# Where 1,024 masked row-maximum instructions put their element-wise result: back into PSUM, or into one SBUF tile

## The chip, the cores and the metric

The kernel runs on one core of a Trainium2 chip. The metric is the device time of one execution in microseconds (us), taken as the median of several executions. A profile of one further execution gives every engine's instructions with their start and duration: PE (TensorE matmuls), PEld (its weight loads), DVE (VectorE), ACT (ScalarE), POOL (GpSimd) and SP (SyncE, which issues most DMAs).

## The reference, cut to what matters

Two layers, each an attention block and a feed-forward block on a sequence of 2048 rows with 640 features:

```python
x = A_x
for layer in range(2):
    x = x + attention(layernorm(x))   # 32 heads of 20; row i sees keys i-255 .. i
    x = x + mlp(layernorm(x))         # 640 -> 1536, relu(.)**2, -> 640, with biases
```

`attention` is softmax(mask(q k^T) / sqrt(20)) v, then a 640x640 projection. The softmax subtracts each row's maximum over its allowed keys. It is these maxima that the change touches.

## The kernel before

**Units.** The sequence is cut into 8 blocks of 256 rows; with two layers that makes 16 units, 0 to 15. Units 0 and 8 are the first of a layer and have no previous block of keys. Each unit goes through stages: layer norm and transposition, q and k (`stage_qk`), v (`stage_v`), attention, output projection (`stage_o`), second layer norm, feed-forward (`stage_f`). The dense stages of the unit before and the unit after are interleaved with the attention of the current unit, so that PE always has something to do.

**Attention.** The 32 heads go in 8 groups of four, called quads. For a quad `max_quad` (L617) first computes raw scores into two PSUM tiles `bb0` and `bb1` of three banks each (PE L653, or L668 in units 0 and 8). Then DVE adds the mask and takes the row maxima: eight reductions (L633), for four pieces w and, within each, for the two tiles e = 0 and 1 in turn. Such a reduction is one `tensor_tensor_reduce`; the profile shows it as two instructions, CUSTOM_DVE_ANT_0 (the pass over the scores, 128x320 in most units, 128x128 and 128x256 in units 0 and 8) and DVE_READ_ACCUMULATOR2_ANT (128x1, which writes the maximum into the small tile `mx`). Before the change the pass wrote the masked scores back over the raw ones, in place. Nothing reads them afterwards: only `mx` is used.

Later `exp_quad` (L737) computes transposed scores into the same two PSUM tiles (PE L757, or L765 where the unit is 0 or 8), with the row maxima included as extra rows of `qt`; ACT takes the exponentials (L779) into `pt`, POOL zeroes the masked corners (L794, L798), and `pv_quad` (L814) multiplies by v (PE L828). `max_quad` runs three quads ahead of `exp_quad`. So the two PSUM tiles change hands all the time: maxima of one quad, exponentials of another, maxima again.

**From the maxima to `qt`.** After every second quad the 16 columns of `mx` are turned into rows. In units 0 and 1 `max_out` (L715) transposes them on PE (L721), and DVE splits them into two half-precision parts in the tile `mT` (L726, L727). From unit 2 on `max_cross` (L694) splits them into `mh` on DVE (L704, L705), and a transposing DMA on SP (L709) makes the tile `mt`. Four small DMAs (L689) then carry the rows into `qt`.

**Order.** Each engine runs its own instructions in the order in which the program issues them. That order is written by a planner inside the kernel: `post` gives every job an engine, a cost in ns, and the jobs that it depends on; `pump` issues a job when its planned start has come. The plan takes 113 + 1.047 ns per column for a reduction (448 ns for 320 columns), whatever it writes. `banks` (L598) makes the next user of the two score tiles wait, in the plan, for all jobs on them, and dense matmuls fill PE's time until then. Accumulators of the dense stages (`acc`), of `pv` and of transposes share two further PSUM banks (`mm_tile`, L228): a matmul group cannot begin until ACT and DVE have emptied the bank it takes. Semaphores between engines, and between instructions of one engine, are not written in the kernel: the tile framework derives them from which instructions read and write which tile.

**SBUF tiles.** Tiles with the same tag share their buffers; a tile that takes over a buffer waits for the last readers of the one before it.

Of the kernel before, what the change touches and what calls it, by code (L numbers as in the profile page):

```python
# [11 lines left out]
F16 = mybir.dt.float16  # L12
BF16 = mybir.dt.bfloat16
# [3 lines left out]
P = 128  # L17
Q = P // 2
# [27 lines left out]
def kernel(ctx: ExitStack, tc: tile.TileContext, x, wqkv, wo, w1, b1, w2, b2, out):  # L46
    nc = tc.nc
# [3 lines left out]
    sb = ctx.enter_context(tc.tile_pool(name="sb", bufs=1))  # L51
# [81 lines left out]
    def post(eng, cost, fn, *deps, wait=0.0, prio=1, **kw):  # L133

        j = Job(eng, cost, fn, [d for d in deps if d is not None], now[0] + wait, prio, **kw)
        k = len(pend)
        while k and pend[k - 1].prio > prio:
            k -= 1
        pend.insert(k, j)
        return j  # L140
# [5 lines left out]
    def dma(fn, size, *deps, n=1, cost=450.0, prio=1, **kw):  # L146

        return post("S", n * cost, fn, *deps, prio=prio, size=size, **kw)
# [18 lines left out]
    def need(*js):  # L167

        for j in js:
            while j.end is None:  # L170
                pass_time()
            now[0] = max(now[0], j.end)
# [55 lines left out]
    def mm_tile(shape, name):  # L228


        while len(banks2) > 1:
            empty = [b for b in banks2 if b and all(j.end is not None for j in b)]
            if empty:
                b = min(empty, key=lambda b: max(j.end for j in b))
                now[0] = max(now[0], max(j.end for j in b) + LAT)
                banks2.remove(b)
            else:
                pass_time()
        t = ps.tile(shape, F32, name=name, tag="mm", bufs=2)
        banks2.append([])  # L240
        return t, banks2[-1]
# [350 lines left out]
    for m in mhs:  # L592
        nc.vector.memset(m, 0.0)

    bbjobs = []
    bb6 = [ps.tile([P, 3, 512], F32, name=f"bb{e}") for e in range(2)]

    def banks():  # L598
        need(*bbjobs)
        bbjobs.clear()  # L600
        return bb6

    def quarters(u):

        return u % NG != 0

    def by_tiles(pieces):

        at, order = {}, []
        for k, (tile, cols, put) in enumerate(pieces):  # L610
            order.append((at.get(tile, 0), k, put))
            at[tile] = at.get(tile, 0) + cols
        for _, _, put in sorted(order, key=lambda o: o[:2]):
            for e in range(2):
                put(e)

    def max_quad(n):  # L617

        u, qd = divmod(n, NQ)
        g = u % NG  # L620
        qt, cur, prev = qts[u], kts[u % 3], kts[(u - 1) % 3]
        G = qd // GQ
        if (u, G) not in mxs:
            mxs[u, G] = sb.tile([P, 2, 2 * GQ, 2], F32, name="mx", bufs=2)
        mx = mxs[u, G]
        need(trips[u, 0, qd], trips[u, 1, qd])
        bb = banks()

        accum = {(e, w): mx[:, e, (2 * qd + w // 2) % (2 * GQ), w % 2:w % 2 + 1] for e in range(2) for w in range(4)}

        def reduce(e, w, v, mask, cols):
            bbjobs.append(post("D", 113 + 1.047 * cols, lambda:
                               nc.vector.tensor_tensor_reduce(out=v, in0=v, in1=mask, scale=1.0, scalar=-3.0e38,  # L633
                                                              op0=ALU.add, op1=ALU.max, accum_out=accum[e, w]),
                               prio=urgency["turn"]))

        if quarters(u):
            flat = [b.rearrange("p a n -> p (a n)") for b in bb]
            pieces = []
            for w in range(4):  # L640
                j, i = divmod(w, 2)
                p, at = 2 * qd + j, 5 * Q * w
                cuts = sorted({0, 5 * Q, *(z - at for z in (512, 1024) if 0 < z - at < 5 * Q)})
                for o0, o1 in zip(cuts, cuts[1:]):
                    for h in range(2):
                        for kt, lo, hi, to in ((prev, 0, T - i * P, i * P), (cur, T - i * P, 3 * P, i * P - T)):
                            a, b = max(lo, o0 + h * Q), min(hi, o1 + h * Q)
                            if a >= b:
                                continue

                            def put(e, kt=kt, a=a, b=b, to=to, h=h, p=p, i=i, o=at + a - h * Q):
                                r, rows = slice(64 * e, 64 * e + 3 * DH), slice(64 * h, 64 * (h + 1))
                                nc.tensor.matmul(flat[e][rows, o:o + b - a], qt[r, p, i * P + 64 * h:i * P + 64 * (h + 1)],  # L653
                                                 kt[r, p, a + to:b + to], start=True, stop=True,
                                                 tile_position=(64 * e, 64 * h))

                            pieces.append((h, b - a, put))
            by_tiles(pieces)
            now[0] += 763.0
            for w in range(4):  # L660
                for e in range(2):
                    reduce(e, w, flat[e][:, 5 * Q * w:5 * Q * (w + 1)], maskq, 5 * Q)
        else:
            for w in range(4):
                j, i = divmod(w, 2)
                for e in range(2):
                    r, p = slice(64 * e, 64 * e + 3 * DH), 2 * qd + j
                    nc.tensor.matmul(bb[e][:, w % 3, w // 3 * T:w // 3 * T + (1 + i) * P], qt[r, p, i * P:(i + 1) * P],  # L668
                                     cur[r, p, :(1 + i) * P], start=True, stop=True)
            now[0] += 440.0  # L670
            for w in range(4):
                j, i = divmod(w, 2)
                for e in range(2):
                    to = bb[e][:, w % 3, w // 3 * T:w // 3 * T + (1 + i) * P]
                    if i:
                        reduce(e, w, to, maskw, 2 * P)
                    else:
                        reduce(e, w, to, maskw[:, P:], P)
        mxjobs[u, G] = list(bbjobs)
# [3 lines left out]
    def rows_out(qt, G, mT, ready):  # L683

        def spread():
            for e in range(2):
                for a in range(2):
                    r = 64 * e + 3 * DH + a
                    nc.sync.dma_start(qt[r:r + 1, 2 * GQ * G:2 * GQ * (G + 1), :].rearrange("p n (i m) -> p (n i) m", i=2),  # L689
                                      mT(e, a))  # L690

        return dma(spread, 16384, ready, n=4, cost=600.0, prio=0)

    def max_cross(u, G):  # L694

        mx, jobs = mxs.pop((u, G)), mxjobs.pop((u, G))
        NR = 8 * GQ
        box = {}

        def split():  # L700
            flat = mx.rearrange("p e n i -> p (e n i)")
            box["m"] = whole = mhs[G % 2]
            m = whole[:, :2 * NR].rearrange("p (a n) -> p a n", a=2)
            nc.vector.tensor_scalar(m[:, 0], flat, -1.0 / MS, None, op0=ALU.mult)  # L704
            nc.vector.scalar_tensor_tensor(m[:, 1], flat, -1.0 / MS, m[:, 0], op0=ALU.mult, op1=ALU.subtract)  # L705

        def turn():
            box["t"] = sb.tile([P, P], F16, name="mt", bufs=1)
            nc.sync.dma_start_transpose(box["t"], box["m"])  # L709

        j = post("D", 220, split, *jobs, prio=0)
        j = dma(turn, P * 2 * NR * 2, j, cost=1250.0, land=CROSS, prio=0)
        rowjobs[u, G] = rows_out(qts[u], G, lambda e, a: box["t"][a * NR + e * NR // 2:a * NR + (e + 1) * NR // 2, :], j)

    def max_out(u, G):  # L715

        qt, mx = qts[u], mxs.pop((u, G))
        NR = 8 * GQ
        need(*mxjobs.pop((u, G)))
        tr, jobs = mm_tile([P, 4, P], "tr")  # L720
        nc.tensor.transpose(tr[:NR, 0, :], mx.rearrange("p e n i -> p (e n i)"), ident)  # L721
        now[0] += 220.0
        mT = sb.tile([NR, 2, P], F16, name="mT", bufs=1)

        def rows():
            nc.vector.tensor_scalar(mT[:, 0], tr[:NR, 0, :], -1.0 / MS, None, op0=ALU.mult)  # L726
            nc.vector.scalar_tensor_tensor(mT[:, 1], tr[:NR, 0, :], -1.0 / MS, mT[:, 0],  # L727
                                           op0=ALU.mult, op1=ALU.subtract)

        j = post("D", 520, rows, prio=0)  # L730
        jobs.append(j)
        rowjobs[u, G] = rows_out(qt, G, lambda e, a: mT[4 * GQ * e:4 * GQ * (e + 1), a, :], j)
# [551 lines left out]
```

## Time and profile before

| | |
|---|---|
| time, median of 3 executions | 1586.17 us (1585.07 to 1589.79) |
| the profiled execution's own time | 1588.33 us |
| its span, first to last instruction | 1586.6 us |
| granted TensorE clock over the span | 0.995 |
| DVE instructions of L633 | 1,024 passes, 1,024 accumulator reads |

The profile's page gives for each engine the time it was busy and its share of the span. A row of the groups reads: line, engine, operation, output tile and input tile, shapes, count, then the total busy time, the mean duration of one instruction in ns, and the idle time of the engine just ahead of these instructions with what ended it. A row of the timeline reads: start in us from the span's start, duration in us, engine, line, operation, tiles, count, and in brackets an idle gap ahead of it with what ended that gap. Neighbouring instructions of the same form are merged into one timeline row. A duration includes any time in which the instruction was already in the engine behind another one, so two rows of one engine can overlap.

### The profile page before, as it was taken

The numbers are of one execution on the slowest core, as the hardware profiler recorded it, in microseconds if no ns is written. First come the engines' busy times: TensorE is split into PE (matmuls) and PEld (weight loads), VectorE is DVE, ScalarE is ACT, GpSimd is POOL, SyncE is SP. The second block draws the span as 40 slices with busy tenths as digits, with TensorE's granted clock in tenths as the row PEclk, the third lists the DMA queues.
The fourth block names the chain that finished last, engine by engine and source line by source line (L and its number), as shares of the span: only waits on it lengthen the run. The fifth ranks groups of instructions, "written<-read, shape, count | busy, mean of one in ns | idle before, by whom it ended". The sixth has DMA issues, their size and how long they took to land. (4 is left out here: it accounts for less than half of the span.)

```text
span 1586.6 us, 52541 instructions
## 1 busy us (share of the span) xinstructions
PE 1558.1 (98%) x21570; PEld 1168.7 (74%) x21570; DVE 984.7 (62%) x3254; ACT 734.3 (46%) x1593; POOL 600.3 (38%) x1291
## 2 busy tenths in 40 slices
PE   8899999999999999999999999999999999999989
PEld 7666777777777777777777777777778777676767
DVE  8776665666756656565566656657665666756532
ACT  4455545444454444535443453444535345354512
POOL 1233534235253443524324252442525325254512
PEclk9998999999999999999999999999999999999999
DMA  9764343362533525354352534535343343431020
GB/s 272 191 181 117 77 107 86 96 131 55 122 87 103 111 57 127 78 124 90 91 132 64 121 87 110 104 70 128 68 125 83 97 111 69 114 87 58 29 67 18
DMA packets 243353, 160.44 MB, mean 101 GB/s; under 512 B 91176, under 2 KB 226856, under 8 KB 243112
## 3 DMA queue, kind: packets, MB, share of 16 engines
q1 hardware_dynamic: 236744, 147.58, 38.8%
q10 hardware_dynamic: 6368, 9.50, 2.1%
q8 instruction: 169, 2.77, 0.7%
q14 instruction: 72, 0.59, 0.1%
HBM read 84.68 MB, written 52.95 MB: 87 GB/s over the span
## 5 line engine op out<-in xcount | busy, mean ns | idle before, releaser
L779 ACT ACTIVATE pt<-bb 128x512 f32<-128x512 f32 (+1 forms) x736 | 376.0, 600 | 227.0 <-PE bb L757 197.8
L633 DVE CUSTOM_DVE_ANT_0 bb<-bb,maskq 128x320 f32<-128x320 f32 x896 | 409.2, 524 | 86.8 <-PE bb L653 74.6
L794 POOL TENSOR_SCALAR_AFFINE_SELECT pt<-pt 128x256 f32<-128x256 f32 x448 | 188.0, 422 | 563.1 <-ACT pt L779 550.3
L327 PE MATMUL acc<-y,w_s 128*128 128x256 f16 x2880 | 328.3, 273 | 2.5 <-ACT y L377 1.4
L327 PE MATMUL acc<-w_s,hh 128*128 128x320 f16 (+1 forms) x2340 | 326.1, 297 | 0.0
L327 PEld LDWEIGHTS <-w_s 128*128 128x128 f16 x2880 | 276.5, 98 | 54.4 <-issue 18.1
L327 PEld LDWEIGHTS <-hh 128*128 128x128 f16 x2340 | 222.1, 98 | 96.8 <-issue 11.5
L327 PEld LDWEIGHTS <-wq_s 128*128 128x128 f16 x2400 | 229.9, 98 | 46.3 <-issue 13.5
L327 PE MATMUL acc<-yT,wq_s 128*128 128x256 f16 x2250 | 258.6, 273 | 2.2 <-DVE qd L510 0.8
L798 POOL TENSOR_SCALAR_AFFINE_SELECT pt<-pt 128x256 f32<-128x256 f32 x512 | 213.7, 439 | 93.0 <-ACT pt L779 91.6
L1013 DVE TENSOR_TENSOR hh<-r,hh 128x256 f16<-128x256 f32 x192 | 95.1, 517 | 208.8 <-ACT hh L1010 201.8
L828 PE MATMUL pv<-pt,vt 128*32 128x128 f32 (+1 forms) x3840 | 190.9, 331 | 1.2 <-POOL pt L798 1.2
L1007 POOL TENSOR_TENSOR r<-r 128x256 f32<-128x256 f32 x192 | 114.2, 615 | 161.2 <-ACT r L1003 158.8
L840 ACT COPY ot<-pv 128x256 f32<-128x256 f32 x128 | 47.7, 373 | 268.8 <-PE pv L828 268.7
L327 PE MATMUL acc<-wo_s,od 128*128 128x320 f16 x960 | 141.7, 303 | 4.8 <-ACT od L911 3.0
L633 DVE DVE_READ_ACCUMULATOR2_ANT mx<- 128x1 f32 x1024 | 145.1, 142 | 0.0
L828 PEld LDWEIGHTS pv<-pt,vt 128*32 128x32 f32 x3840 | 105.4, 110 | 41.7 <-POOL pt L798 6.5
L327 PE MATMUL acc<-wq_s,yT 128*128 128x320 f16 x900 | 132.0, 299 | 1.4 <-DVE y L378 0.9
L327 PEld LDWEIGHTS <-od 128*128 128x128 f16 x960 | 92.1, 99 | 51.0 <-issue 6.4
L1003 ACT ACTIVATE r<-acc,b1s 128x256 f32<-128x256 f32 x192 | 80.7, 472 | 87.7 <-PE acc L327 86.4
L327 PEld LDWEIGHTS <-yT 128*128 128x128 f16 x900 | 85.7, 98 | 39.3 <-issue 6.7
L364 POOL TENSOR_TENSOR bmv<-bmv,neghalf 128x1 f32<-128x1 f32 x64 | 45.5, 717 | 136.1 <-DVE bmv L358 135.7
(95 smaller groups left out, 1226.3 us busy)
## 6 DMA issues: line engine op xcount, KB each, us to landing
qt<-qk SPq DMA_DIRECT2D x30, 480.0 KB
kt<-qk SPq DMA_DIRECT2D x30, 480.0 KB
qk<-qd SPq DMA_DIRECT2D x17, 640.0 KB
o<-ot SPq DMA_DIRECT2D x256, 42.0 KB
od<-o SPq DMA_DIRECT2D x14, 640.0 KB
qk<-yl SPq DMA_DIRECT2D x13, 640.0 KB
qk<-qd SPq DMA_DIRECT2D x17, 320.0 KB
xt<-in_A_x_dram SPq DMA_DIRECT2D x16, 320.0 KB
```

Of the source, the lines that this page charges most:

```text
L327: nc.tensor.matmul(acc, lhs(a, c), rhs(b, c), start=(k == 0), stop=(k == 3 * nk - 1))
L364: j = post("G", 520, lambda: nc.gpsimd.tensor_tensor(box["mv"][:, 3:4], box["mv"][:, 2:3], neghalf, op=ALU.pow), j, prio=prio)
L633: nc.vector.tensor_tensor_reduce(out=v, in0=v, in1=mask, scale=1.0, scalar=-3.0e38, op0=ALU.add, op1=ALU.max, accum_out=accum[e, w]),
L779: nc.scalar.activation(box["pt"][:, :o], bb[e][:, k, :o], AF.Exp, scale=SCALE / (QS * QS))
L794: nc.gpsimd.affine_select(out=m, in_=m, pattern=[[0, 2], [-1, P]], compare_op=ALU.is_gt, fill=0.0, base=0, channel_multiplier=1)
L798: nc.gpsimd.affine_select(out=m, in_=m, pattern=[[0, 2], [1, P]], compare_op=ALU.is_ge, fill=0.0, base=0, channel_multiplier=-1)
L828: nc.tensor.matmul(pv[32 * jj:32 * (jj + 1), q0 * P:(q0 + qn) * P], vf[:, c:c + 32], pj[:, j, :], start=(k == 0), stop=(k == len(steps) - ...
L840: nc.scalar.copy(ot[:, qd % 2], pv)
L1003: nc.scalar.activation(box["r"], acc[:, f, :], AF.Relu, bias=b1s[:, f0 + f:f0 + f + 1], scale=1.0 / (YS * WS))
L1007: nc.gpsimd.tensor_tensor(box["r"], box["r"], box["r"], op=ALU.mult)
L1013: nc.vector.tensor_sub(hh[:, 1, f, :], box["r"], hh[:, 0, f, :])
```

## The change

The reductions write their masked scores to a new SBUF tile `junk`, one tile for all 1,024 of them, in bfloat16, instead of over the float32 scores in PSUM. The maxima still go to `mx` in float32. Beside that, the tile `mT` of units 0 and 1 and the tile `mt` of the later units get one tag, so they share one buffer.

```diff
+    junk = sb.tile([P, 5 * Q], BF16, name="junk")
     bbjobs = []
     bb6 = [ps.tile([P, 3, 512], F32, name=f"bb{e}") for e in range(2)]
...
         def reduce(e, w, v, mask, cols):
             bbjobs.append(post("D", 113 + 1.047 * cols, lambda:
-                               nc.vector.tensor_tensor_reduce(out=v, in0=v, in1=mask, scale=1.0, scalar=-3.0e38,
+                               nc.vector.tensor_tensor_reduce(out=junk[:, :cols], in0=v, in1=mask, scale=1.0, scalar=-3.0e38,
                                                               op0=ALU.add, op1=ALU.max, accum_out=accum[e, w]),
...
         def turn():
-            box["t"] = sb.tile([P, P], F16, name="mt", bufs=1)
+            box["t"] = sb.tile([P, P], F16, name="mt", tag="mt", bufs=1)
             nc.sync.dma_start_transpose(box["t"], box["m"])
...
-        mT = sb.tile([NR, 2, P], F16, name="mT", bufs=1)
+        mT = sb.tile([NR, 2, P], F16, name="mT", tag="mt", bufs=1)
```

`junk` is 128 partitions by 320 columns of two bytes. No instruction is added or removed in the program's text, and the planner's costs are unchanged.

## The prediction

> **What bounds the kernel now.** I read the page's first part, then the table by stretches of time, then the waits of PE.
>
> ```profile
> span 1586.6 us, 52541 instructions
> PE 1558.1 (98%) x21570; PEld 1168.7 (74%) x21570; DVE 984.7 (62%) x3254; ACT 734.3 (46%) x1593; POOL 600.3 (38%) x1291
> 0.00:97.00 97.00, 86.85 (x842) 64.49 (x842) 74.39 (x256) 48.19 (x98) 18.66 (x44) 0.96 0.84 226
> 394.00:491.00 97.00, 97.00 (x1448) 73.20 (x1440) 60.01 (x198) 45.29 (x98) 38.23 (x84) 1.00 0.42 97
> PE bb L653 <- ACT pt L779: 4.1, 6, 1.9
> PE tr L721 <- DVE mx L633: 0.2, 1, 0.2
> ```
>
> In the stretches the first number after the length is PE's busy time, the third is DVE's. From 394 to 491 us, a stretch of one unit, PE is busy for all of its 97.00 us while DVE works 60.01. Over the span PE stands still for 1586.6 - 1558.1 = 28.5 us. In the list of PE's waits the longest is 4.1 us, and a wait for a reduction (`mx`, L633) appears with 0.2 us. So PE sets the time, and faster reductions can win next to nothing. What matters is the opposite: whether the reductions become later, and how much later they may be before PE notices.
>
> **Part 1: the pass itself.** I compare the groups that read float32 from PSUM and a second operand from SBUF.
>
> ```profile
> L633 DVE CUSTOM_DVE_ANT_0 bb<-bb,maskq 128x320 f32<-128x320 f32 x896 | 409.2, 524 | 86.8 <-PE bb L653 74.6 <-issue 10.5 <-ACT pt L779 1.1
> L633 DVE DVE_READ_ACCUMULATOR2_ANT mx<- 128x1 f32 x1024 | 145.1, 142 | 0.0
> L939 DVE SCALAR_TENSOR_TENSOR x<-acc,x 128x320 f32<-128x320 f32 x60 | 29.3, 488 | 30.5 <-PE acc L327 28.7 <-DMA x<-in_A_x_dram 1.3 <-DMA qk<-qd 0.4
> L510 DVE SCALAR_TENSOR_TENSOR qd<-acc,qd 128x512 f16<-128x512 f32 x36 | 24.9, 691 | 59.7 <-ACT qd L507 59.5
> L510 DVE SCALAR_TENSOR_TENSOR qd<-acc,qd 128x256 f16<-128x256 f32 x18 | 7.5, 416 | 0.7 <-ACT qd L507 0.7
> ```
>
> L939 has the size of a reduction but writes to SBUF: 488 ns, against 524 for the reduction into PSUM. Two-byte output does not shorten it: L510, which writes float16 to SBUF, takes 691 ns for 512 columns and 416 for 256, so 1.07 ns per column and 485 for 320. The timeline explains the 36 ns of difference.
>
> ```profile
> 708.18 0.48 DVE L939 SCALAR_TENSOR_TENSOR x<-acc,x 128x320 f32<-128x320 f32 x1
> 708.58 0.48 DVE L633 CUSTOM_DVE_ANT_0 bb<-bb,maskq 128x320 f32<-128x320 f32 x1
> 708.98 0.14 DVE L633 DVE_READ_ACCUMULATOR2_ANT mx<- 128x1 f32 x1
> 708.98 0.53 DVE L633 CUSTOM_DVE_ANT_0 bb<-bb,maskq 128x320 f32<-128x320 f32 x1
> 709.43 0.14 DVE L633 DVE_READ_ACCUMULATOR2_ANT mx<- 128x1 f32 x1
> 712.12 0.14 DVE L633 DVE_READ_ACCUMULATOR2_ANT mx<- 128x1 f32 x1
> ```
>
> The first reduction of this batch takes 0.48, as long as L939. The second begins while the first one's accumulator read is under way and shows 0.53: 0.05 of it is that read. So the place of the output costs nothing that these rows show, and I take 0 for it. The ends are 0 and 36 ns less per reduction, 1,024 x 36 ns = 37 us of DVE time, of which PE would see nearly nothing by the waits above.
>
> **Part 2: the new order among reductions.** The same rows show that the reductions overlap now. The second begins 0.40 us after the first, and then they follow at (712.12 - 708.98) / 7 = 0.45 us, though each lasts about 0.5. They may, because neighbours write different PSUM tiles (e = 0, then e = 1); the reduction of the same tile is two places back. With the change all of them write the same columns of `junk`, each over the one before. Does the program then make each wait for the one before? Two places show what an ordered pair of DVE instructions looks like.
>
> ```profile
> 167.65 2.10 DVE L96 MEMSET kt<- 128x512 f32 x4 [0.17 <-DVE w_s L260]
> 700.50 0.49 DVE L633 CUSTOM_DVE_ANT_0 bb<-bb,maskq 128x320 f32<-128x320 f32 x1
> 700.90 0.14 DVE L633 DVE_READ_ACCUMULATOR2_ANT mx<- 128x1 f32 x1
> 701.08 0.18 DVE L704 TENSOR_SCALAR mh<-mx 128x16 f16<-128x16 f32 x1
> ```
>
> At 167.65 a fill of a K tile stands behind DVE's own L260, which only read that tile: overwriting is ordered by a semaphore on one engine too. I take it that writing over a write is treated the same. And L704, which reads the last maximum, shows the price: it starts 0.58 us after the reduction that it waits for, namely 0.40 to the accumulator read, 0.14 for it, and 0.04 until the wait is over. So with the change the spacing becomes 0.58 in place of 0.45, or 0.13 more for each of the seven steps inside a batch: **0.91 us per batch of eight**. The 128 batches hold 116 us of it. DVE has 1586.6 - 984.7 = 601.9 us to spare, so it does not become the bound as a whole; the question is which batches are late. Bounds for the price of a step: 0, if no wait is made or it costs nothing, and 0.14 + 0.04 = 0.18, if the accumulator read and the gap come whole on top of today's 0.45; I take 0.13, the difference of two measured spacings.
>
> The Trainium skill has a rule against this: its page "VectorE: DVE Perf Modes", section "The DRAIN you can't avoid", says that eight copies took as long with a semaphore after each as with one at the end, "the semaphore costs nothing extra here". By that rule the sum below would be 0 and the time that of before. This trace disagrees for these instructions: 0.58 behind a wait against 0.45 without.
>
> **Part 3: what waits behind a late batch.** Behind the reductions on DVE stand the evictions of the dense accumulators (L510, L939) and the other DVE work, and on PE the next score matmuls (L757), which take over the two PSUM tiles. I go through the eight batches of one steady unit. Its worst place:
>
> ```profile
> 696.64 0.50 DVE L633 CUSTOM_DVE_ANT_0 bb<-bb,maskq 128x320 f32<-128x320 f32 x1 [1.10 <-PE bb L653]
> 699.29 0.53 DVE L633 CUSTOM_DVE_ANT_0 bb<-bb,maskq 128x320 f32<-128x320 f32 x1
> 699.89 0.69 DVE L510 SCALAR_TENSOR_TENSOR qd<-acc,qd 128x512 f16<-128x512 f32 x1
> 700.70 1.25 PE L327 MATMUL acc<-wq_s,yT 128*128 128x320 f16 x8
> ```
>
> Seven reductions stand ahead of the eviction L510. The seventh would start at 696.64 + 6 x 0.58 = 700.12, and L510 0.40 behind it, at 700.52 instead of 699.89: 0.63 late. It ends at 700.58 now, and PE begins the group that needs the bank at 700.70. Of these 0.12 some 0.04 are the semaphore, so PE loses 0.63 - 0.08 = 0.55. The second place is a batch that other work has split, so that only its last five reductions are neighbours:
>
> ```profile
> 723.68 0.49 DVE L633 CUSTOM_DVE_ANT_0 bb<-bb,maskq 128x320 f32<-128x320 f32 x1
> 725.43 0.53 DVE L633 CUSTOM_DVE_ANT_0 bb<-bb,maskq 128x320 f32<-128x320 f32 x1
> 725.88 0.14 DVE L633 DVE_READ_ACCUMULATOR2_ANT mx<- 128x1 f32 x1
> 726.18 0.75 PE L757 MATMUL bb<-qt,kt 62*64 62x192 f16 x32
> 714.00 0.75 PE L757 MATMUL bb<-qt,kt 62*64 62x192 f16 x32
> 665.16 0.14 DVE L633 DVE_READ_ACCUMULATOR2_ANT mx<- 128x1 f32 x1
> 666.16 0.75 PE L757 MATMUL bb<-qt,kt 62*64 62x192 f16 x32
> ```
>
> Four steps now take 725.43 - 723.68 = 1.75, and would take 2.32: 0.57 late. The last read ends at 726.02, PE starts at 726.18: it loses 0.57 - 0.12 = 0.45. The first of the last three rows belongs to the batch from 708.58: its reductions end at 712.26 and PE comes at 714.00, a slack of 1.74 us that swallows 0.91 whole. The last two are the batch with the next smallest slack, 666.16 - 665.30 = 0.86: it loses 0.1. The other four, read in the same way, have 1.24 to 2.01 and lose nothing. A steady unit thus loses **1.1 us**, and 12 units (2 to 13) 13 us.
>
> In unit 1 and in the last stretch the slack is smaller. One batch of the first kind and one of the second:
>
> ```profile
> 174.96 0.14 DVE L633 DVE_READ_ACCUMULATOR2_ANT mx<- 128x1 f32 x1
> 175.21 0.75 PE L757 MATMUL bb<-qt,kt 62*64 62x192 f16 x32
> 1420.34 0.14 DVE L633 DVE_READ_ACCUMULATOR2_ANT mx<- 128x1 f32 x1
> 1420.59 0.75 PE L757 MATMUL bb<-qt,kt 62*64 62x192 f16 x32
> 39.09 0.27 PE L721 MATMUL tr<-ident,mx 128*16 128x128 f32 x1 [0.22 <-DVE mx L633]
> ```
>
> In both the slack is 0.11, and PE would lose 0.91 - 0.07 = 0.84. Read batch by batch, the 9 of unit 1 (97 to 200 us) have slacks from 0.03 to 2.2 and lose about 0.5 each, 4.5 us; the 13 from 1360 us on have, but for one, slacks from 0 to 0.53 and lose 7 us in all. In the first 97 us PE already waits on DVE, as the last row shows, so that most of the delay passes through: 11 batches at about 0.65 make 7 us. **The sum is 13 + 4.5 + 7 + 7 = 31.5 us.** From the profiled execution's own 1588.3 this makes 1619.8; that execution lies 2.2 us above the median of the runs shown, so I forecast 1617.6.
>
> **Part 4: the shared small tile.** Its two users meet once, when `mt` first takes over from `mT`:
>
> ```profile
> 176.54 2.75 SPq L689 DMA_DIRECT2D qt<-mT  x4
> 200.60 1.15 SPq L709 DMA_TRANSPOSE mt<-mh  x1
> ```
>
> The last reads of `mT` are issued by 176.54 + 2.75 = 179.29, the first `mt` is filled at 200.60. These 21 us cover the reads' landing, so the wait costs nothing; without that cover it would hold SP, with all DMAs queued behind it, for the time of one small DMA. In each kind by itself the buffer turned over as before.
>
> **Rivals.**
> - *The waits cost nothing, or aren't made.* Against it stand the L96 and L704 rows; for it, that DVE writes in order and the pair needs no protection. The spacing stays at 0.45 or falls to the 0.40 of L939, and since PE hardly waits for reductions, the time stays within 2 us of 1586. This is the not-slower side, and it holds from a step price of about 0.02 us downwards, where every slack but the smallest covers seven steps.
> - *Everything passes through.* If the dense evictions behind each batch have as little slack as the L510 at 699.89, PE loses the full 0.91 in 128 batches: 1586 + 116 = 1702 us. Against it is the measured slack of 1.24 to 2.01 us in five of a steady unit's eight batches; a partial form, where late evictions delay ACT and from there the exponentials, would give some 1635 to 1650.
> - *PE gains from a PSUM that DVE no longer writes.* Nothing speaks for it: PE is fully busy in stretches with and without reductions. At most the 0.2 us of waits for L633 and a few us of the 28.5 idle could go: 1582.
>
> **How the numbers follow.** Forecast by late batches, 1600 to 1635: 0.66. Partial or full pass-through above that: 0.15, of which 0.06 above 1650. No cost: 0.15. A gain: 0.04. A measurement of this kernel can tell about 0.3%, 4.8 us, from no change. Slower by more than that: 0.66 + 0.15 = 0.81; within: 0.15; faster: 0.04. The range runs from 1586, half of the no-cost case, to 1650; that leaves out about 0.04 + 0.07 + 0.06.
>
> **What would show it.** In the profile of the changed kernel the reductions of a batch should follow each other at 0.58 us with a recorded 0.49 each, the next one beginning behind the accumulator read and not with it. DVE's idle time ahead of L633 should name L633 itself, some 100 us. PE's waits should gain about 30 us, named L633 (by L757) and L510 (by the dense groups), most in the first 200 and the last 230 us, and the steady unit should last 1.1 us longer. If the spacing is still 0.45, part 2 is wrong; if the spacing is 0.58 but the steady unit is several us longer, part 3 is wrong, in the evictions.

## The result and the profile after

| | before | after |
|---|---|---|
| median | 1586.17 us (1585.07 to 1591.43, 5 runs) | 1604.40 us (1603.20 to 1605.03, 5 runs) |
| profiled execution, own time | 1588.33 us | 1603.20 us |
| its span | 1586.6 us | 1601.5 us |

The change makes the kernel slower: ratio 1.0105, 95% interval 1.0091 to 1.0119, 18 us. The forecast was 1617.6 us in a range of 1586 to 1650; the direction and the range held, and the loss is 0.58 of the 31.5 us that were predicted.

The first part of the page after:

```profile
span 1601.5 us, 52602 instructions
PE 1562.7 (98%) x21570; PEld 1171.0 (73%) x21570; DVE 1009.9 (63%) x3254; ACT 734.3 (46%) x1593; POOL 603.4 (38%) x1291
```

The two groups of the reductions on DVE, by form, after (line numbers are one higher than before, L634 for L633; the columns are the busy time in us and the mean ns of one, then DVE's idle time just before them and what ended it):

```profile
L634 DVE CUSTOM_DVE_ANT_0 junk<-bb,maskq 128x320 bf16<-128x320 f32 x896 | 439.1, 490 | 124.3 <-PE bb L654 85.0 <-DVE mx L634 5.9 <-ACT pt L780 1.1
L634 DVE DVE_READ_ACCUMULATOR2_ANT mx<- 128x1 f32 x1024 | 84.3, 82 | 0.1
```

A pass is now recorded with 490 ns instead of 524, and an accumulator read with 82 instead of 142. Taken alone each instruction has become shorter, and yet the kernel is slower: means of durations say nothing about when the next one may start. The idle time ahead of the reductions rose from 86.8 to 124.3 us. That is visible in the order of time. One batch of eight on DVE after the change, the same one that began at 708.58 before:

```profile
713.79 0.47 DVE L634 CUSTOM_DVE_ANT_0 junk<-bb,maskq 128x320 bf16<-128x320 f32 x1
714.19 0.08 DVE L634 DVE_READ_ACCUMULATOR2_ANT mx<- 128x1 f32 x1
714.41 0.49 DVE L634 CUSTOM_DVE_ANT_0 junk<-bb,maskq 128x320 bf16<-128x320 f32 x1
714.83 0.08 DVE L634 DVE_READ_ACCUMULATOR2_ANT mx<- 128x1 f32 x1
714.95 0.49 DVE L634 CUSTOM_DVE_ANT_0 junk<-bb,maskq 128x320 bf16<-128x320 f32 x1
...
718.03 0.08 DVE L634 DVE_READ_ACCUMULATOR2_ANT mx<- 128x1 f32 x1
718.03 0.48 DVE L940 SCALAR_TENSOR_TENSOR x<-acc,x 128x320 f32<-128x320 f32 x1
```

The second pass no longer begins with the first one's accumulator read (714.19) but 0.14 behind its end, at 714.41; from the third on the spacing is 0.53 (714.41 to 714.95). L940 at the end of the batch does not touch `junk`, and it begins in the same moment as the last read. So the gap belongs to the pair of reductions, not to DVE. From the first start to the end of the last read the batch takes 718.11 - 713.79 = 4.32 us; before it took 712.26 - 708.58 = 3.68. A batch is 0.64 us longer.

That waits were added can also be counted. A separate wait is an EVENT_SEMAPHORE instruction of DVE's sequencer (DVEq) ahead of a pass. Those of the reductions, before and after:

```profile
L633 DVEq EVENT_SEMAPHORE  x141: 21/21/5833, 51.7 to 1487.0; - x141
L634 DVEq EVENT_SEMAPHORE  x202: 21/21/5292, 31.7 to 1502.1; - x101
```

These 61 more waits are the whole difference between the 52541 and 52602 instructions of the two profiles.

PE notices after the change in two places. The first is a dense group behind a late eviction. The group and the one ahead of it, on PE, first as they stood before (the second group at 700.70 is in the prediction) and then after:

```profile
697.96 2.90 PE L327 MATMUL acc<-yT,wq_s 128*128 128x256 f16 x25
```

```profile
702.76 2.90 PE L327 MATMUL acc<-yT,wq_s 128*128 128x256 f16 x25
705.91 1.25 PE L327 MATMUL acc<-wq_s,yT 128*128 128x320 f16 x8 [0.24 <-DVE qd L510]
```

The batch and the eviction behind it, on DVE after the change:

```profile
701.44 0.49 DVE L634 CUSTOM_DVE_ANT_0 junk<-bb,maskq 128x320 bf16<-128x320 f32 x1 [1.10 <-PE bb L654]
705.17 0.69 DVE L510 SCALAR_TENSOR_TENSOR qd<-acc,qd 128x512 f16<-128x512 f32 x1
```

The second place is the score matmuls behind a batch that is split. The first and the last of its five neighbouring reductions after the change, and the score matmuls:

```profile
728.88 0.48 DVE L634 CUSTOM_DVE_ANT_0 junk<-bb,maskq 128x320 bf16<-128x320 f32 x1
731.43 0.08 DVE L634 DVE_READ_ACCUMULATOR2_ANT mx<- 128x1 f32 x1
731.38 0.93 PE L758 MATMUL bb<-qt,kt 62*64 62x192 f16 x32
```

These are the two places that the prediction named. The dense group starts 3.15 us behind the group ahead of it (702.76 to 705.91) instead of 2.74 (697.96 to 700.70): 0.41 us lost, of which the bracket shows 0.24 as standstill. At 731.38 the score matmuls start before the last reduction is read, and the group takes 0.93 instead of 0.75 us: 0.18 lost inside it. The waits of PE that grew most, all of them for reductions or for the eviction behind them (in all, times, longest, us):

```profile
PE acc L327 <- DVE qd L510: 3.6, 14, 0.4
PE bb L758 <- DVE mx L634: 2.2, 7, 0.6
PE bb L766 <- DVE mx L634: 1.4, 4, 0.5
```

Before, the first of these stood at 0.8 us and the other two did not appear. PE's whole standstill, span less busy time, rose from 28.5 to 38.8 us.

The length of a steady unit is read from the first score matmul of one unit to that of the next (units 4 and 5), before and then after:

```profile
369.52 0.30 PE L653 MATMUL bb<-kt,qt 60*64 60x256 f16 x4
466.09 0.30 PE L653 MATMUL bb<-kt,qt 60*64 60x256 f16 x4
```

```profile
372.59 0.30 PE L654 MATMUL bb<-kt,qt 60*64 60x256 f16 x4
469.74 0.30 PE L654 MATMUL bb<-kt,qt 60*64 60x256 f16 x4
```

96.57 us became 97.15, or 0.58 more.

### The profile page after: what moved, and what is told of

Read it like the earlier page. It is cut to its first block, busy times and chain, and to the rows that moved or that the text cites. A ratio compares the mean times of both kernels' runs of the same rounds, so it can differ in the third digit from the quotient of the medians.

```text
span 1601.5 us, 52602 instructions
## 1 busy us (share of the span) xinstructions
PE 1562.7 (98%) x21570; PEld 1171.0 (73%) x21570; DVE 1009.9 (63%) x3254; ACT 734.3 (46%) x1593; POOL 603.4 (38%) x1291
## 4 chain that ended last, share of the span: by engine, by line
PE 82%; DVE 10%; ACT 2%; DMA 2%; issue 2%; SPq 1%; POOL 1%; DVEq 0%; ACTq 0%; POOLq 0%
PE acc L327 64%; PE pv L829 9%; DVE junk L634 6%; PE bb L758 5%; PE bb L654 4%; ACT pt L780 1%; DVE qd L510 1%; DMA qk<-qd 1%; DMA x<-in_A_x_dram 1%; SPq L690 0%; PE bb L669 0%; DVE hh L1014 0%; PE bb L766 0%; ACT r L1004 0%; DMA o<-ot 0%
## 5 line engine op out<-in xcount | busy, mean ns | idle before, releaser
L634 DVE CUSTOM_DVE_ANT_0 junk<-bb,maskq 128x320 bf16<-128x320 f32 x896 | 439.1, 490 | 124.3 <-PE bb L654 85.0
L327 PEld LDWEIGHTS <-hh 128*128 128x128 f16 x2340 | 222.1, 98 | 96.8 <-issue 11.5
L758 PE MATMUL bb<-qt,kt 62*64 62x64 f16 (+3 forms) x3552 | 89.4, 234 | 3.5 <-DVE mx L634 2.2
```

What stands on the lines that cost most here:

```text
L327: nc.tensor.matmul(acc, lhs(a, c), rhs(b, c), start=(k == 0), stop=(k == 3 * nk - 1))
L634: nc.vector.tensor_tensor_reduce(out=junk[:, :cols], in0=v, in1=mask, scale=1.0, scalar=-3.0e38, op0=ALU.add, op1=ALU.max, accum_out=accum ...
L758: nc.tensor.matmul(bb[e][rows, k, o + a:o + b], kt[r, 2 * qd + j, ko + 64 * h:ko + 64 * (h + 1)], qt[r, 2 * qd + j, q0 * P + a:q0 * P + b] ...
```

## The experiments

The theory to test (**wait**): all reductions write one tile, so each has to wait until the one ahead has finished, and batches end late. Its rival (**destination**): writing to SBUF, or in two bytes, is what costs. The third suspect is the shared small tile.

**The price of a pair by itself.** A small kernel with rows of 24 equal DVE instructions of 320 columns, back to back (its calls, shortened):

```python
red(out=v, in0=v)                  # L47: in place, two PSUM tiles in turn
red(out=bb0, in0=bb0)              # L50: in place, one PSUM tile
red(out=jk[0], in0=v)              # L52: one bfloat16 SBUF tile
red(out=jk[k % 2], in0=v)          # L54: two in turn
red(out=jf, in0=v)                 # L58: one float32 SBUF tile
scalar_tensor_tensor(jk[0], v)     # L60: one tile;  L62: four in turn
tensor_copy(jk[0], mask)           # L64: one tile;  L66: four in turn
```

> Leaves out the whole computation (it copies input rows to the output) and runs ten rows of 24 DVE instructions of 320 columns back to back. Wait theory, spacing from start to start: reductions in place on two PSUM tiles in turn 0.45, on one PSUM tile 0.58; into one bfloat16 SBUF tile 0.53, into two or four in turn 0.40 to 0.45, into one float32 SBUF tile 0.53; scalar_tensor_tensor from PSUM into one SBUF tile 0.50 to 0.55, into four in turn 0.40; copies SBUF to SBUF into one tile longer by 0.05 to 0.15 than into four in turn. Rule of the Trainium skill that a semaphore after each costs nothing: each pair the same.

The rows of its lines; behind the count stand the shortest, median and longest duration in ns, then the first and the last start in us:

```profile
L47 DVE CUSTOM_DVE_ANT_0 bb<-bb,mask x24: 500/528/531, 5.4 to 16.3; 128x320 f32<-128x320 f32 x24
L50 DVE CUSTOM_DVE_ANT_0 bb<-bb,mask x24: 498/499/526, 16.7 to 30.3; 128x320 f32<-128x320 f32 x24
L52 DVE CUSTOM_DVE_ANT_0 jk<-bb,mask x24: 490/491/492, 30.9 to 43.2; 128x320 bf16<-128x320 f32 x24
L54 DVE CUSTOM_DVE_ANT_0 jk<-bb,mask x24: 484/485/491, 43.7 to 53.2; 128x320 bf16<-128x320 f32 x24
L58 DVE CUSTOM_DVE_ANT_0 jf<-bb,mask x24: 484/491/492, 63.5 to 75.7; 128x320 f32<-128x320 f32 x24
L60 DVE SCALAR_TENSOR_TENSOR jk<-bb,mask x24: 487/491/492, 76.2 to 88.2; 128x320 bf16<-128x320 f32 x24
L62 DVE SCALAR_TENSOR_TENSOR jk<-bb,mask x24: 477/477/491, 88.7 to 97.9; 128x320 bf16<-128x320 f32 x24
L64 DVE COPY jk<-mask x24: 229/244/245, 98.3 to 104.7; 128x320 bf16<-128x320 bf16 x24
L66 DVE COPY jk<-mask x24: 232/236/244, 105.0 to 108.5; 128x320 bf16<-128x320 bf16 x24
```

The distance from first to last start, divided by 23, is the spacing. Into PSUM: 0.59 us on one tile (L50) against 0.45 on two in turn (L47, where one gap of 1.07 for the second tile's matmul is left out). Into SBUF: 0.53 on one tile, in either type (L52, L58), 0.41 on two (L54). Without an accumulator: 0.52 against 0.40 (L60, L62). Copies within SBUF: 0.28 against 0.15 (L64, L66). In every pair the instruction lasts the same to within 30 ns; only the start moves, by 0.12 to 0.14 us. SBUF is the cheaper destination (0.41 against 0.45), so the destination theory has the sign wrong.

This bears on the rule that the prediction weighed. The Trainium skill's page "VectorE: DVE Perf Modes", section "The DRAIN you can't avoid", has eight copies take the same time with and without a semaphore after each. In these rows copies are nearly twice as far apart when each overwrites the last one's tile, 0.28 against 0.15 us. The trace's records tell the two apart: all 24 copies on one tile and 21 of the 24 on four tiles wait for DVE's own semaphore, but on four tiles the last writer of the tile is four places back and done by then. The copies there that carry no wait are 0.15 apart as well. So a semaphore as such costs nothing that these rows show, and waiting for the instruction just ahead costs 0.13.

**Taking the wait out of the kernel.** Two tiles, or the second one in PSUM as before:

```diff
-    junk = sb.tile([P, 5 * Q], BF16, name="junk")
+    junk = [sb.tile([P, 5 * Q], BF16, name=f"junk{e}") for e in range(2)]
...
-                               nc.vector.tensor_tensor_reduce(out=junk[:, :cols], in0=v, ...
+                               nc.vector.tensor_tensor_reduce(out=junk[e][:, :cols], in0=v, ...
```

The second tile's 640 bytes per partition come from the scratch for dynamic DMAs (1024 to 256 bytes).

> Two junk tiles, one for e = 0 and one for e = 1, so neighbouring reductions write different tiles and the one of the same tile is two places back; output still bfloat16 in SBUF. Wait theory: spacing inside a batch 0.40 to 0.45 us, time as before the change, 1583 to 1589 us. Destination theory (writing to SBUF is what costs): time as changed, 1600 to 1606 us.

Measured 1584.59 us; ratio to before 0.9985 (0.9974 to 0.9995). This is no longer slower than before, and faster by a hair.

```profile
703.56 0.48 DVE L634 CUSTOM_DVE_ANT_0 junk<-bb,maskq 128x320 bf16<-128x320 f32 x1
703.97 0.08 DVE L634 DVE_READ_ACCUMULATOR2_ANT mx<- 128x1 f32 x1
703.97 0.48 DVE L634 CUSTOM_DVE_ANT_0 junk<-bb,maskq 128x320 bf16<-128x320 f32 x1
704.38 0.08 DVE L634 DVE_READ_ACCUMULATOR2_ANT mx<- 128x1 f32 x1
704.38 0.48 DVE L634 CUSTOM_DVE_ANT_0 junk<-bb,maskq 128x320 bf16<-128x320 f32 x1
```

Here each pass begins with the accumulator read of the one before, 0.41 apart. The other form needs no second tile:

```diff
-    out=junk[:, :cols]
+    out=junk[:, :cols] if e == 0 else v
```

> Reductions of e = 0 write to junk, those of e = 1 in place in PSUM as before the change; the SBUF space is that of the changed kernel. Wait theory: neighbours write different tiles, no wait that binds, 1583 to 1589 us. Destination theory: half the SBUF writes, half the loss, 1594 to 1597 us.

Measured 1584.94 us, ratio 0.9983 (0.9973 to 0.9994). Half of the writes go to SBUF, and nothing of the loss is left.

**Putting the wait into the kernel before,** with no SBUF write at all:

```diff
-            for w in range(4):
-                for e in range(2):
+            for e in range(2):
+                for w in range(4):
                     reduce(e, w, flat[e][:, 5 * Q * w:5 * Q * (w + 1)], maskq, 5 * Q)
```

> The kernel before, in place in PSUM, but the four reductions of e = 0 come first and then the four of e = 1 (units 1 to 7 and 9 to 15), so each writes the tile that the one ahead has just written. Wait theory: spacing 0.58 us for six of seven steps, batch 0.7 to 0.8 us longer, slower than before by 12 to 30 us (1598 to 1616). Destination theory: no SBUF write, so 1584 to 1589 us.

Measured 1608.30 us, ratio 1.0129 (1.0113 to 1.0145). The timeline shows the waits inside one tile, and none where the tile changes (718.31, with the read):

```profile
716.71 0.50 DVE L633 CUSTOM_DVE_ANT_0 bb<-bb,maskq 128x320 f32<-128x320 f32 x1
717.12 0.14 DVE L633 DVE_READ_ACCUMULATOR2_ANT mx<- 128x1 f32 x1
717.30 0.50 DVE L633 CUSTOM_DVE_ANT_0 bb<-bb,maskq 128x320 f32<-128x320 f32 x1
...
717.89 0.50 DVE L633 CUSTOM_DVE_ANT_0 bb<-bb,maskq 128x320 f32<-128x320 f32 x1
718.31 0.14 DVE L633 DVE_READ_ACCUMULATOR2_ANT mx<- 128x1 f32 x1
718.31 0.53 DVE L633 CUSTOM_DVE_ANT_0 bb<-bb,maskq 128x320 f32<-128x320 f32 x1
```

The four pieces `w` of a tile are columns of their own, so the wait is for the tile, not for a value that would be overwritten too early. With that the wait theory holds in both directions, and the destination theory falls.

**The remaining parts of the change.** The tags of `mt` and `mT` taken back, with one junk tile kept (here and in the next run with the smaller scratch of the kernel with two tiles):

```diff
-            box["t"] = sb.tile([P, P], F16, name="mt", tag="mt", bufs=1)
+            box["t"] = sb.tile([P, P], F16, name="mt", bufs=1)
...
-        mT = sb.tile([NR, 2, P], F16, name="mT", tag="mt", bufs=1)
+        mT = sb.tile([NR, 2, P], F16, name="mT", bufs=1)
```

> One junk tile as in the change, but mT and mt keep buffers of their own (the 256 bytes come from a smaller scratch for dynamic DMAs). Wait theory: the shared small tile has no part in it, so as changed, 1602 to 1607 us. Theory that the sharing costs: faster than the changed kernel by its part, down to 1586 us.

Measured 1604.48 us, ratio 1.0111 (1.0097 to 1.0125): the sharing costs nothing, nor is it the smaller scratch that made the two tiles fast. Then the one tile in float32:

```diff
-    junk = sb.tile([P, 5 * Q], BF16, name="junk")
+    junk = sb.tile([P, 5 * Q], F32, name="junk")
```

> The changed kernel with the one junk tile in float32 instead of bfloat16 (same scratch reduction). Wait theory: type plays no part, spacing 0.53, 1602 to 1607 us. Theory that the conversion to two bytes is what costs: 1584 to 1590 us.

Measured 1603.64 us, ratio 1.0104 (1.009 to 1.0117): the type plays no part.

**Which units pay.** The one tile in some units alone, in place elsewhere (here units 0 and 1; likewise `2 <= u < 14` and `u >= 14`):

```diff
-    out=junk[:, :cols]
+    out=junk[:, :cols] if u < 2 else v
```

> One junk tile for the maxima of units 0 and 1 alone, the others in place as before the change. Wait theory as predicted for the first two units (7 + 4.5 us): ratio to before 1.007, about 1599 us. Wait theory as the two profiles compare at 180 us (before and after the change only 0.3 us apart there): ratio 1.000. Seen against the profile with two junk tiles, which is 6.6 us ahead there: ratio 1.003 to 1.004.

> One junk tile for the maxima of units 2 to 13 alone. Predicted: 12 units of 1.1 us, 13 us, ratio 1.008. By the two profiles (8.5 us from the maxima of unit 2 to those of unit 14): ratio 1.005.

> One junk tile for the maxima of units 14 and 15 alone. Predicted 7 us, by the two profiles 6.1 us: ratio 1.004. If the loss at the end were only handed on from earlier units: ratio 1.000.

| junk tile in | ratio to before | 95% interval | of 1587.7 us | predicted |
|---|---|---|---|---|
| units 0 and 1 | 1.0033 | 1.002 to 1.0045 | 5.2 us | 11.5 us |
| units 2 to 13 | 1.0056 | 1.0044 to 1.0069 | 8.9 us | 13 us |
| units 14 and 15 | 1.002 | 1.001 to 1.003 | 3.2 us | 7 us |

The three add up to 17.3 us; all units together cost 1.05% of the same time, 16.7. So the stretches pay side by side, within what the intervals allow; no part was found that arises only when all are late. The last stretch came out at half of what both the prediction and the comparison of the two profiles (6.1 us) gave.

Between the two profiles the first units had looked free: unit 2's first score matmul came at 179.91 before and 180.18 after. The kernel before was therefore profiled once more.

> The kernel before, unchanged, for a second profile of its first 200 us, where the first one shows a granted clock of 0.90 from 100 to 150 us. If the clock made that start slow, the maxima of unit 2 begin at 174 to 177 us instead of 179.9; if not, at 179 to 181.

Two rows from unit 0, the stretch from 100 to 150 us (behind its length PE's busy time, then the other engines'; the 0.90 or 0.97 is the granted clock) and that matmul, first of the first profile, then of the second:

```profile
47.75 0.49 PE L765 MATMUL bb<-qt,kt 62*128 62x256 f16 x7 [1.50 <-DMA qt<-mT]
50.80 0.82 PE L668 MATMUL bb<-kt,qt 60*128 60x128 f16 x8
100.00:150.00 50.00, 43.42 (x566) 29.46 (x564) 39.72 (x113) 24.62 (x51) 16.71 (x31) 0.90 0.57 155
179.91 0.76 PE L653 MATMUL bb<-kt,qt 60*64 60x256 f16 x38
```

```profile
46.71 0.49 PE L765 MATMUL bb<-qt,kt 62*128 62x256 f16 x7 [1.00 <-DVE bmv L358]
48.87 0.50 PE L668 MATMUL bb<-kt,qt 60*128 60x128 f16 x8
100.00:150.00 50.00, 42.55 (x572) 29.33 (x568) 40.02 (x119) 23.63 (x49) 16.76 (x31) 0.97 0.56 149
176.64 0.76 PE L653 MATMUL bb<-kt,qt 60*64 60x256 f16 x38
```

Unit 2 begins 3.3 us earlier here, at the time that was expected if the clock had made the first start slow. The rows show that the clock from 100 to 150 us cannot be the main reason: 1.0 us of the lead is there in the first row (46.71 against 47.75, where PE stands 1.50 us for a DMA into `qt`), and 1.9 us in the second. How the rest divides was not separated. Nothing of the lead is left at the end: the two executions took 1588.33 and 1588.53 us. Against the second profile the changed kernel is 3.5 us late at unit 2, inside the interval of the timed runs (3.2 to 7.1 us). One profile of the start, where the arrival of DMAs and the clock vary, does not suffice for a few microseconds.

**Telling the planner.** The planner still takes 448 ns for a reduction. Two attempts to correct it failed, both against what I expected.

```diff
-            bbjobs.append(post("D", 113 + 1.047 * cols, lambda:
+            bbjobs.append(post("D", 198 + 1.047 * cols, lambda:
```

> The changed kernel with the planner told what a reduction now takes, 198 + 1.047 ns per column (533 ns for 320, the measured spacing) instead of 113 + 1.047. Wait theory with the loss made by batches that come later than planned: PE gets dense matmuls to fill the gap and most of the loss returns, 1587 to 1598 us. Theory that the loss is DVE work that nothing can cover: 1601 to 1608 us.

Measured 1641.56 us, ratio 1.0349 (1.0335 to 1.0363): 37 us worse than the change itself. Its longest wait of PE:

```profile
PE acc L327 <- DVE od L915: 20.8, 14, 2.6
```

Before, PE waited 1.8 us in all for L914, the same line. The new order reaches the output projection before its input is split. These waits are some 19 us longer than before the change, about half of the 37; the rest was not traced. The other attempt, in the kernel with two tiles, set the cost to the 0.411 us measured there:

```diff
-            bbjobs.append(post("D", 113 + 1.047 * cols, lambda:
+            bbjobs.append(post("D", 76 + 1.047 * cols, lambda:
```

> Two junk tiles, and the planner told the spacing measured with them, 0.411 us for 320 columns (76 + 1.047 ns per column). Wait theory: PE is the bound and already fed, so little is left: 1580 to 1587 us, at most 3 us below two junk tiles alone. If the plan's 37 ns per reduction had mattered: below 1578 us.

Measured 1598.98 us, ratio 1.0073 (1.006 to 1.0085), 14 us worse than two tiles alone. Nearly all of this is there when unit 1 begins: its first score matmul comes at 97.49 us, and at 83.82 with two tiles alone. The timeline has a new standstill of PE in unit 0:

```profile
64.38 0.76 PE L669 MATMUL bb<-kt,qt 60*128 60x128 f16 x8 [3.24 <-ACT pt L780]
```

How this standstill and the rest of the loss follow from the new cost stays open. What is shown is that a truer cost in one place of this plan changes the order of all engines, and cost more in both cases than the error that it removed.

## Why the prediction was right, and where its sizes were off

- **What bounds the kernel:** right. With two tiles DVE's reductions come 0.41 apart instead of 0.45, and the kernel gains only 0.15%: PE has no use for them.
- **Part 1, the destination costs nothing:** right for the pass, which is as long into SBUF as into PSUM to within 10 ns where nothing overlaps it (L52 and L50 of the small kernel), but it missed the accumulator read. It takes 0.08 us behind a pass into SBUF and 0.14 behind one into PSUM (the rows of the accumulator reads, L634 above and L633 in the prediction). The prediction looked at the pass's own row alone.
- **Part 2, the wait is made:** right, and this is the term that was mis-sized. Its price was taken from the row of L704 behind a PSUM reduction, 0.58, and so contains the longer read. (The 0.45 beside it was not "without" a wait: by the trace's records a pass there also waits for DVE's semaphore, but for the pass two places back, which is done.) The spacing is 0.53, the step 0.08 instead of 0.13 us. One thing was not foreseen: the first step of a batch is longer, 0.62 instead of 0.53 (713.79 to 714.41). The second reduction of a batch is the first one on the other score tile, so that it has PE to wait for as well as DVE. The trace agrees: a separate wait instruction stands ahead of the second pass in all 101 batches whose first two passes of 320 columns are neighbours, and the step there is 0.63 us in 62 of them and 0.67 in the 39 that also wait for ACT (medians), against 0.53 in the 633 steps without one. No run took the second wait away. From read to read, a batch's first step grew by 0.19 (0.45 to 0.64, 714.19 to 714.83) and the six others by 0.51 together (2.69 to 3.20); the last read is 0.06 shorter. That makes the 0.64 us per batch that were measured, in place of 0.91.
- **Part 3, who waits behind a batch:** right in a steady unit, in its places and in the slacks that it read. Behind the batch's first reduction, L510 now comes after 3.73 us (701.44 to 705.17) instead of 3.25 (696.64 to 699.89), so it is 0.48 late and not 0.63; less the slack of 0.08 that is 0.40, and PE lost 0.41. The split batch takes 2.63 us (728.88 to 731.51) instead of 2.34 (723.68 to 726.02), so it is 0.29 late; less the slack of 0.12 that is 0.17, and the score group is 0.18 longer. The third place, priced at 0.1, is covered. With the measured steps the prediction's own sum is thus 0.57 us for the unit in place of 1.1, and 0.58 was measured. The stretches at both ends were scaled up from a few rows, and paid 5.2 and 3.2 us instead of 11.5 and 7. The shorter batch, taken in proportion, is a factor of 0.64/0.91 = 0.70; that would make 22 us of 31.5. It covers the steady units (9.1 for 13, and 8.9 measured); the other 4 to 5 us are the two ends, where "most of the delay passes through" was too much. Which slacks there were misjudged was not traced.
- **Check on the price:** in the reordered kernel a wait in PSUM does cost what the prediction took, 0.59 from start to start, and a batch is 6 x 0.14 = 0.86 us longer, near the 0.91. Its steady unit is 0.88 us longer (first score matmuls at 373.89 and 471.34), where 1.1 was predicted. Its 20.5 us in all are not the price of the whole prediction, because units 0 and 8 keep the old order there.
- **Part 4, the shared tile:** right, 1604.48 against 1604.40 us without and with it.
- **What would show it:** the passes of 0.49 and their start behind the read came as described. DVE's idle time ahead of the reductions grew by 37.5 us and names L634 with only 5.9, not 100: by the prediction's own row of L704 only 0.04 us lie between a read and the next pass, gaps that short are not named in the list, and only some of those in front of a second pass appear. PE's waits were to gain about 30 us and gained 10.3; the ones named L634 or L510 in the list above gained 6.4 of them. Of the 14.9 us between the two spans 4.6 are not standstill but matmuls that last longer, as the group at 731.38 does. Most of the waits were to lie in the first 200 and the last 230 us; the two ends have 8.4 of the 17.3 us of loss.
- **The rivals:** "the waits cost nothing" is refuted by the rows of the small kernel, "everything passes through" by the 0.58 us of a steady unit, whose eight batches are 5.1 us longer together.

## What to carry to other kernels

A scratch output that nobody reads is still a write: if every instruction writes the same tile, each is held until the one before has finished, 0.12 to 0.14 us a piece in the small kernel, and two tiles in turn avoid it. What such a delay costs is not its sum (by estimate 82 us, if all 128 batches were longer by the 0.64 of the one read above) but what is left of it after the slack of each place; the kernel lost 17 to 18 us. Read the spacing of starts, not the mean duration: here both durations of a reduction fell and the kernel became slower.

## What the runs showed that was not expected

- An accumulator read behind a pass into SBUF takes 0.082 us, behind one into PSUM 0.14, so two reductions into different tiles can follow each other at 0.41 us in SBUF and at 0.45 in PSUM.
- Copies of 320 bfloat16 columns within SBUF last 0.24 us each, yet start 0.15 us apart when they write four tiles in turn; on one tile they start 0.28 apart.
- Waits follow the tile and not the columns: in the reordered kernel reductions into separate columns of one tile start 0.59 us apart, though none overwrites the one ahead.
